# Block pairs 1 to 5 of tiles 2 to 6 by seven products; strided attention output in halves of one PSUM bank

## The chip, the cores and the metric

The kernel runs on one core of one Trainium2 chip. The metric is device time in microseconds (us) of one execution. All times are for the whole kernel; a profiled execution is also split by instruction and by engine: PE (matrix multiply), PEld (its weight loads), DVE (vector), ACT (scalar), POOL, and SP, which here only issues DMAs.

## What is computed

Sparse attention on 8 batches, 8 heads, 576 positions and a head size of 64, followed by a bilinear feed-forward layer on the 8 x 576 = 4608 tokens:

```python
mask_local = (rel >= 0) & (rel < 32)                                  # heads 0 to 3
mask_strided = (rel >= 0) & (pos[None, :] % 32 == pos[:, None] % 32)  # heads 4 to 7
scores = np.where(masks, scale * q @ k.T, -1e9)
attn = softmax(scores)
x = (attn @ v).transpose(0, 2, 1, 3).reshape(4608, 512)
out = ((x @ w_a) * (x @ w_b)) @ w_out        # w_a, w_b: 512 x 1536, w_out: 1536 x 512
```

## The kernel before

**Tiles and slots.** The feed-forward layer works on nine tiles of 512 tokens, t = 0 to 8. A tile has 16 slots: twelve for the blocks f of 128 of the 1536 columns (a and b are computed, and their product goes as bf16 into `pf`), and four for the output y. The attention of batch b is computed a tile ahead: its steps are spread over the slots of tile b-1. An order written out by hand decides where; each engine does its instructions in that order. `steps` maps a position to names of steps, `take(position)` issues them. A position is a slot (16t + slot, at the slot's end), or a place inside a slot: `("p", t, g)` late in block pair g, `("y", t, n)` after the n-th finished part of the output.

**Block pairs.** Blocks 2g and 2g+1 form pair g. An ordinary block takes four matmuls of 512 columns for a and four for b (L625), an ACT copy of a to SBUF (L646) and a DVE multiplication (L649). In tiles 2 to 6, pairs 1 to 4 (`MID_A`) go through `a_pair_mid`: the four matrix quarters of the pair's a come from seven products (of sums of quarters of x, in `xsum`, and of w_a, in `wsum_a`) instead of eight. A product is two matmuls of 256 columns, `P(...)` at L695; four products add up in the bank X, which ACT copies to SBUF after each (L721, L724, L731, L738), one is in Y and two are in Z. DVE adds the quarters (L717, three times a pair) and multiplies with the two banks b1 and b0 (L714, twice); b still takes eight matmuls of 512 columns (L709). Tiles 7 and 8 have a variant of their own, `a_pair`.

**PSUM banks.** `mm_bank` deals four banks in turn (three named mm and one named tp), so that a bank comes back after four. A pair takes four of them and the bank `e`; which of the five serves as X, Y, Z, b1, b0 changes with g in a cycle of three (L687). The output takes the next three.

**Attention steps of batch b in tile b-1.** Units u = 0 to 3 are the local heads, 4 to 7 the strided ones. `Q` copies transposed queries, `S` computes scores with their exponentials (on PE and ACT) and masks them (DVE); `s` and `m` are its two parts. `V` is the output. For u = 0 to 3: six matmuls into bank `o`, a reciprocal (L468), and a product into `xl` (L486), then by DMA (`O`, `I`) into `xT`. For u = 4 to 7, `step_VT`: eight matmuls of 72 columns (L519), four into `o` and four into `e`; on ACT a logarithm of each half (L531) and one exponential of both (L532), for the reciprocal of the sums; two DVE products into `xT` (L534). In tiles 2 to 6 the order is `PAIRED`, with V4 at slot 9, V5 at slot 11, and S7, V6 and V7 inside the output (`IN_Y`).

**Output.** y comes from seven products, too, on the two token halves i of `pf`, in two parts q each: 14 chains of six matmuls of 256 columns (L895), in the order `Y_ORDER`. Products 7, 6, 5 and 3 use the sums s2, s1, s0, s3 of `pf` quarters, which `fast_s` puts into `pss` on DVE (L829) piece by piece from slot 9 on. Products 1, 6, 5, 3 add up in one bank, 7 and 4 in a second, 2 is in a third; ACT copies after 1, 7, 6, 5 and 3 (L860, L866), DVE adds for 4, `+` and 2.

**The rest.** `wsum_make` (L668) makes the w_a sums on DVE: groups 1 to 4 in slots 17 to 19, groups 0 and 5 in slots 44 to 47. `pace` (L1146) is a one-element POOL copy of what the slot has finished: it holds back the DMAs that POOL issues behind it. SP issues the transposing loads (`step_D`: L322, L325, L328).

Of the kernel before, what the change touches and what calls it, by code (L numbers as in the profile page):

```python
# [7 lines left out]
F32 = mybir.dt.float32  # L8
BF16 = mybir.dt.bfloat16
# [7 lines left out]
RS = 8  # L17
# [10 lines left out]
FAST_Y = (1, 2, 3, 4, 5, 6, 7, 8)  # L28
MID_A = {t: (1, 2, 3, 4) for t in (2, 3, 4, 5, 6)}
FAST_A = {7: (1, 2, 3, 4, 5), 8: (0, 1, 2, 3, 4, 5)}  # L30
# [3 lines left out]
def kernel(  # L34
# [473 lines left out]
    def step_VT(b, u):  # L508

        c, half, M, n, G = unit(u)  # L510
        p = ps.pop((b, u))
        if "e" in psum4:
            o = [psum4[nm].tile([128, 512], F32, tag=nm, name=nm) for nm in "oe"]
        else:
            o2 = psum4["o"].tile([128, 2, 512], F32, tag="o", name="o")
            o = [o2[:, j] for j in range(2)]
        for j in range(2):
            for i in range(G):
                nc.tensor.matmul(o[j][:, i * n:(i + 1) * n], lhsT=vs_buf[b % 2][:, u - HL, 2 * i + j],  # L519
                                 rhs=p_cols(b, p, j, i, n, n)[:M], start=True, stop=True)  # L520
        r = sb.tile([128, RS * 4 * D], BF16, tag="xr", name="xr", bufs=2)[:64, :4 * W].bitcast(F32)
        by_token = lambda t: t.rearrange("d (p i j) -> d p i j", i=G, j=2)
        dst = xT[64 * (u % 2):64 * (u % 2) + 64, c, S * (b % XR):S * (b % XR + 1)]
        if "e" not in psum4:
            by_j = lambda t: t.rearrange("d j (i p) -> d p i j", p=NP)
            nc.scalar.activation(by_token(r), by_j(o2[64:, :, :W]), ACT.Ln)
            nc.scalar.activation(r, r, ACT.Exp, scale=-1.0)
            nc.vector.tensor_mul(by_token(dst), by_j(o2[:64, :, :W]), by_token(r))
            return
        for j in range(2):  # L530
            nc.scalar.activation(by_token(r)[:, :, :, j], o[j][64:, :W].rearrange("d (i p) -> d p i", p=NP), ACT.Ln)  # L531
        nc.scalar.activation(r, r, ACT.Exp, scale=-1.0)  # L532
        for j in range(2):
            nc.vector.tensor_mul(by_token(dst)[:, :, :, j], o[j][:64, :W].rearrange("d (i p) -> d p i", p=NP),  # L534
                                 by_token(r)[:, :, :, j])

# [29 lines left out]
    def F_mm(f, w, kk):  # L566
# [17 lines left out]
                 30: "V7"}}  # L584
    LATER = {-4: "Q0", -3: "Q1", -1: "S0", 0: "S1", 1: "V0", 2: "S2", 3: "V1 Q2 O0", 4: "S3 Q3", 5: "V2", 6: "S4", 7: "V3 O1 I0", 8: "S5", 9: "V4 I1",
             10: "S6",
             11: "V5"}
    IN_Y = {2: "S7", 6: "V6", 11: "V7"}
    PAIRED = {-4: "Q0", -3: "Q1", -1: "S0", 0: "S1", 1: "V0 Q2", 2: "s2", 3: "V1 Q3 O0", 4: "s3", 5: "V2", 6: "s4", 7: "V3 O1 I0", 8: "s5",
              9: "V4 I1", 10: "s6", 11: "m6 V5"}  # L590
    IN_P = {1: "m2", 2: "m3", 3: "m4", 4: "m5"}
    FN = {"Tk": step_Tk, "Tq": step_Tq, "S": step_S, "V": step_V, "X": step_X, "W": lambda b, n: fast_w(n, slice(0, 3)),
          "s": S_px, "m": S_m, "L": lead_vl, "O": rows_out, "I": rows_in, "Pk": lambda b, c: pair_up("k", c), "Pq": lambda b, c: pair_up("q", c),
          "Q": lambda b, n: step_Q(b, n // 2, n % 2)}
# [87 lines left out]
    def a_pair_mid(t, g):  # L682
# [47 lines left out]
        P(X, ws(0), xs(0))  # L730
        nc.scalar.copy(quarter(1, 1), X)  # L731
        P(Z, w(1, 1), xs(3))
        add(quarter(1, 0), Z)
# [6 lines left out]
        mult(0, b0)  # L740
        if g == 4:
            fast_s(t, 0, slice(0, 4))
        yield pf[:1, 2 * g, :1]
# [75 lines left out]
    def fast_s(t, n, gs):  # L819
        if t not in pss:  # L820
            pss[t] = nat.tile([128, FG * 5 * SW], BF16, tag="shared", name="ps").rearrange("p (n g m) -> p n g m", g=FG, n=5)
        s = pss[t][:, :, gs, :HT]
        x = pfs[t].rearrange("p (g e) (i m) -> p e i g m", e=2, i=2)[:, :, :, gs]
        a, b, op = ((x[:, 0, 1], x[:, 1, 1], ALU.add), (s[:, 0], x[:, 0, 0], ALU.subtract),
                    (x[:, 0, 0], x[:, 0, 1], ALU.subtract), (x[:, 1, 0], s[:, 1], ALU.subtract))[n]
        if (t, n) == (NT - 1, 2) and {gs.start, gs.start + 1} <= set(FAST_A[t]):
            later[t, gs.start] = lambda: nc.gpsimd.tensor_tensor(s[:, n], a, b, op=op)
            return
        nc.vector.tensor_tensor(s[:, n], a, b, op=op)  # L829
# [37 lines left out]

    Y_ORDER = [(x[0], int(x[1])) for x in "10 11 70 71 60 61 40 41 50 51 20 21 30 31".split()]
    TAIL_ORDER = [(x[0], int(x[1])) for x in "10 11 20 60 70 61 50 71 30 40 51 41 31 21".split()]

# [9 lines left out]
    def y_plan(t):  # L880
# [11 lines left out]

        for k, q, g in by_block(Y_ORDER, 2 if late else 0):
            b, lhs, rhs = plan[k]
            nc.tensor.matmul(bank[b][:, q], lhsT=lhs(g, q), rhs=rhs(g), start=k in "172" and q == 0 and g == 0,  # L895
                             stop=g == FG - 1, skip_group_check=True)
            if g == FG - 1:
                if q == 1:
                    y_post(k, y, slice(0, 2), bank[b])
                    if k == "5":  # L900
                        y_post("+", y, slice(0, 2), None)
                take(("y", t, Y_ORDER.index((k, q)) + 1))
            yield y
        do(16 * t + 19, store_half, 0)
# [34 lines left out]
    def ffn_ys(t, j, mid):  # L939
# [6 lines left out]
        if j == 3:  # L946
            for _ in yst[t]:
                pass
        return (y[0][:1, 0, :1], None, y[1][:1, 0, HN:HN + 1], y[1][:1, 0, :1])[j]

# [35 lines left out]
    with tc.manual_schedule(engines={ENG.PE, ENG.SP, ENG.Pool, ENG.DVE, ENG.Activation}):  # L986
# [78 lines left out]
        for b in range(1, B):  # L1065
            for pos, names in (STEPS.get(b) or {16 * (b - 1) + x: n for x, n in (PAIRED if b - 1 in MID_A else LATER).items()}).items():
                steps.setdefault(pos, []).append((b, names.split()))
            if b not in STEPS:
                for g in MID_A.get(b - 1, ()):
                    steps["p", b - 1, g] = [(b, IN_P[g].split())]  # L1070
                for n, names in IN_Y.items():
                    steps["y", b - 1, n] = [(b, names.split())]

# [5 lines left out]
        soon = {}  # L1079
        for t in FAST_Y[:-1]:  # L1080
            if t not in FAST_A:
                soon[16 * t + 10] = [lambda t=t: fast_s(t, 2, slice(4, 6))]
            soon[16 * t + 11] = [lambda t=t, n=n: fast_s(t, n, slice(4, 6)) for n in (0, 1)]
# [22 lines left out]
        for n in range(4):  # L1106
            do((17, 17, 18, 19)[n], wsum_make, n, slice(1, 5))
            do(16 * 2 + 12 + n, wsum_make, n, slice(0, 6, 5))
        for t in MID_A:
# [19 lines left out]
        for t in FAST_Y[:-1]:  # L1129
            for slot, n, z0, z1 in (  # L1130
                    ((8, 0, 0, 4),) if t == 1 else ()) + ((9, 2, 0, 4), (10, 1, 0, 4), (12, 3, 0, 6)) if t == 1 or t in MID_A else ((4, 0, 0, 2), (5, 2, 0, 2), (6, 1, 0, 2), (7, 3, 0, 2), (8, 2, 2, 4), (9, 0, 2, 4),
                                    (10, 1, 2, 4), (12, 3, 2, 6)):
# [47 lines left out]
```

## Time and profile before

| | |
|---|---|
| time, median of 3 runs | 321.34 us (319.42 to 321.73) |
| the profiled execution: time | 319.59 us |
| its span, first to last instruction | 317.9 us |
| granted PE clock, mean of the span | 0.997 |
| PE share of the chain that ended last | 84% |
| time of tiles 2, 3, 4, 5, 6 in the trace | 32.8, 32.9, 33.6, 32.9, 32.8 us |
| DVE busy in these tiles | 29.99, 30.44, 29.75, 29.78, 28.82 us |
| ACT busy in these tiles | 22.30, 22.41, 22.54, 22.38, 22.29 us |

The 1.7 us between span and time lie around the first and last instruction. [...]

### The profile page before, as it was taken

What the parts mean: (1) busy time and instruction counts of PE and PEld (TensorE: products, weight loads), DVE (VectorE), ACT (ScalarE), POOL (GpSimd) and SP (SyncE); (2) the same over time, 40 slices, a digit from 0 to 9 for tenths busy, and PEclk for the clock granted to TensorE, in tenths of its full rate; (3) what the DMA queues carried; (4) which work ended last, traced back from release to release, by engine and by line L of the source; (5) the groups of instructions that cost most, each with busy time, mean ns of one, the idle gap of its engine ahead of it and who ended that gap; (6) DMA issues with size and microseconds to landing.
All of it is one profiled execution on the core that took longest, in us unless ns stands there. A gap on an engine that the chain in (4) does not pass through costs nothing.

```text
span 317.9 us, 7371 instructions
## 1 busy us (share of the span) xinstructions
PE 310.7 (98%) x2798; PEld 220.7 (69%) x2798; DVE 263.9 (83%) x594; ACT 198.4 (62%) x414; POOL 111.5 (35%) x183
## 2 busy tenths in 40 slices
PE   8999999999999999999999999999999999999994
PEld 6754555455866687767988986769676966786684
DVE  5887876698979998999789978997899768857862
ACT  6964766455766776567756866586667755436541
POOL 8935712791264064205430445033101112203520
PEclk9999999999999999999999999999999999999998
DMA  8999999999999999999999999999252040004004
GB/s 152 172 205 194 204 186 204 220 98 165 115 134 169 251 119 78 129 92 209 147 157 230 130 90 102 96 226 155 26 154 58 0 133 2 2 0 133 2 0 134
DMA packets 127059, 40.32 MB, mean 127 GB/s; under 512 B 114864, under 2 KB 124144, under 8 KB 126832
## 3 DMA queue, kind: packets, MB, share of 16 engines
q0 software_dynamic: 79760, 19.20, 67.1%
q1 hardware_dynamic: 47120, 20.59, 35.9%
q8 instruction: 22, 0.36, 0.5%
q14 instruction: 13, 0.11, 0.2%
q10 hardware_dynamic: 144, 0.07, 0.1%
HBM read 38.93 MB, written 18.28 MB: 180 GB/s over the span
## 4 chain that ended last, share of the span: by engine, by line
PE 84%; DVE 6%; DMA 3%; POOL 2%; SPq 2%; issue 2%; ACT 1%; DVEq 0%; POOLq 0%
PE mm L895 19%; PE mm L625 18%; PE mm L709 8%; PE mm L695 6%; PE mm L775 6%; PE st L379 4%; PE mm L957 3%; PE ax L768 3%; PE e L695 2%; PE mm L768 2%; PE o L460 2%; DMA shared<-in_q_dram 2%; PE mm L922 2%; DMA qTs<-qr 2%; SPq L328 1%
## 5 line engine op out<-in xcount | busy, mean ns | idle before, releaser
L1146 POOL CAST pace<-pf 1x1 f32<-1x1 bf16 x47 | 15.2, 324 | 99.7 <-DVE pf L714 53.9
L625 PE MATMUL mm<-xT,wb_sb 128*128 128x512 bf16 (+1 forms) x192 | 47.4, 362 | 0.0
L625 PE MATMUL mm<-xT,wa_sb 128*128 128x512 bf16 (+1 forms) x192 | 47.4, 362 | 0.0
L399 ACT ACTIVATE p<-st 72x576 bf16<-72x576 f32 (+1 forms) x56 | 36.4, 650 | 9.2 <-PE st L379 8.2
L709 PE MATMUL mm<-xT,wb_sb 128*128 128x512 bf16 (+1 forms) x168 | 38.4, 343 | 0.0
L646 ACT COPY a_sb<-mm 128x512 f32<-128x512 f32 x44 | 25.7, 583 | 15.7 <-PE mm L625 14.9
L895 PEld LDWEIGHTS <-ps 128*128 128x128 bf16 x336 | 32.7, 98 | 3.7
L625 PEld LDWEIGHTS <-wb_sb 128*128 128x128 bf16 x192 | 18.2, 98 | 16.9 <-DMA wb_sb<-in_moe_w_b_dram 0.5
L895 PE MATMUL mm<-wf,ps 128*128 128x256 bf16 x252 | 29.8, 273 | 0.0
L860 ACT COPY y_sb<-mm 128x512 f32<-128x512 f32 (+1 forms) x32 | 17.9, 558 | 19.0 <-PE mm L895 16.4
L649 DVE TENSOR_TENSOR pf<-a_sb,mm 128x512 bf16<-128x512 f32 x34 | 23.1, 680 | 5.9 <-ACT a_sb L646 5.7
L775 PE MATMUL mm<-xT,wb_sb 128*128 128x512 bf16 x88 | 26.2, 379 | 0.0
L625 PEld LDWEIGHTS <-wa_sb 128*128 128x128 bf16 x192 | 17.4, 98 | 12.4
L1146 POOL COPY pace<-y_sb 1x1 f32<-1x1 f32 x22 | 8.4, 380 | 49.5 <-DVE y_sb L858 27.0
L895 PEld LDWEIGHTS <-pf 128*128 128x128 bf16 x252 | 23.5, 98 | 2.7
L709 PEld LDWEIGHTS <-wb_sb 128*128 128x128 bf16 x192 | 18.7, 97 | 7.4
L714 DVE TENSOR_TENSOR pf<-a_sb,mm 128x512 bf16<-128x512 f32 x35 | 22.7, 683 | 0.5
L238 POOL DMA_DIRECT2D vs<-in_v_dram x24 | 21.7, 907 | 3.9 <-issue 1.6
L895 PE MATMUL mm<-wo_sb,pf 128*128 128x256 bf16 x168 | 21.8, 273 | 0.0
L829 DVE TENSOR_TENSOR ps<-pf 128x512 bf16<-128x512 bf16 (+2 forms) x37 | 17.8, 481 | 0.7
L417 DVE TENSOR_TENSOR p<-p,mask_l 128x576 int16<-128x576 int16 x32 | 14.4, 450 | 2.2 <-ACT p L399 2.0
L460 PEld LDWEIGHTS <-p 128*128 128x128 bf16 (+1 forms) x256 | 12.9, 97 | 4.7 <-DVE p L417 1.3
(222 smaller groups left out, 735.8 us busy)
## 6 DMA issues: line engine op xcount, KB each, us to landing
out_dram<-y_sb SPq DMA_DIRECT2D x14, 512.0 KB, 5.2
kr<-in_k_dram POOLq DMA_DIRECT2D x12, 288.0 KB, 6.8
qr<-in_q_dram POOLq DMA_DIRECT2D x12, 288.0 KB, 8.1
vl<-in_v_dram POOLq DMA_DIRECT2D x6, 384.0 KB, 8.8
out_dram<-y_sb SPq DMA_DIRECT2D x7, 256.0 KB, 4.4
vs<-in_v_dram POOLq DMA_DIRECT2D x24, 72.0 KB, 5.7
xd<-xl SPq DMA_DIRECT2D x12, 144.0 KB, 5.0
wo_sb<-in_moe_w_out_dram POOLq DMA_DIRECT2D x4, 384.0 KB, 12.0
```

Source lines behind the costliest of these rows:

```text
L238: nc.gpsimd.dma_start(out=vs_buf[b % 2][:, h, :, 0:D], in_=v[b, HL + h].rearrange("(p r) d -> p r d", r=RS))
L399: nc.scalar.activation(p_flat(p)[:M, :2 * W].rearrange("p (i n) -> p i n", n=2 * n), st[:M].rearrange("p a (i n) -> p (a i) n", n=256)[:, ...
L460: nc.tensor.matmul(of[:, j, i, :w], lhsT=pt, rhs=vt, start=True, stop=True)
L625: nc.tensor.matmul(ps_[:, c0:c0 + n], lhsT=w[:, kk, 128 * f:128 * (f + 1)], rhs=xT[:, kk, x0:x0 + n], start=(kk == first and c0 == 0), sto ...
L646: nc.scalar.copy(a_sb, ab[0])
L649: nc.vector.tensor_mul(pf[:, f, :].rearrange("p (i a s) -> p a i s", i=2, s=16), halves(a_sb), halves(ab[1]))
L695: nc.tensor.matmul(bank, lhsT=lhs(c), rhs=rhs(c), start=start and c == 0, stop=c == 1, skip_group_check=True)
L709: nc.tensor.matmul(dst, lhsT=wb_sb[:, kk, 128 * f:128 * (f + 1)], rhs=rhs, start=kk == 0 and k in (None, 0), stop=kk == KD - 1 and k in (N ...
L714: nc.vector.tensor_mul(pf[:, 2 * g + e, :].rearrange("p (i a s) -> p a i s", i=2, s=16), halves(a[e]), halves(bank))
L775: nc.tensor.matmul(got[e], lhsT=wb_sb[:, kk, 128 * f:128 * (f + 1)], rhs=xT[:, kk, x0:x0 + TTOK], start=kk == 0, stop=kk == KD - 1)
L895: nc.tensor.matmul(bank[b][:, q], lhsT=lhs(g, q), rhs=rhs(g), start=k in "172" and q == 0 and g == 0, stop=g == FG - 1, skip_group_check=True)
L1146: nc.gpsimd.tensor_copy(pace, done)
```

## The change

Five things. (1) Pair 5 of tiles 2 to 6 also goes through `a_pair_mid`. (2) In these tiles the outputs of the strided units are computed in halves: `VT_p` does four matmuls into one bank (`o` or `e`), one logarithm and one exponential, `VT_n` one DVE product. There are eight halves; they stand inside pairs 4 and 5 (`("q", t, g)`, a new place behind the copy of the X bank's third product) and inside the output, at `("m", t, n)`, after n output matmuls. (3) The output's products come in another order, `MID_ORDER`: product 2's first part is drawn forward beside product 1. (4) The sums of `pf` are made in five larger instructions instead of seven; s0 and s3 are made inside the output, and s1 is formed from s2. Q0 and Q1 move to places inside the output of the tile before. `pace` looks at the two halves of y in the other order. (5) The w_a sums of group 5 are made together with those of groups 1 to 4.

```diff
@@ -26,7 +26,7 @@
 FAST_Y = (1, 2, 3, 4, 5, 6, 7, 8)
-MID_A = {t: (1, 2, 3, 4) for t in (2, 3, 4, 5, 6)}
+MID_A = {t: (1, 2, 3, 4, 5) for t in (2, 3, 4, 5, 6)}
 FAST_A = {7: (1, 2, 3, 4, 5), 8: (0, 1, 2, 3, 4, 5)}
@@ -509,11 +509,8 @@
         p = ps.pop((b, u))
-        if "e" in psum4:
-            o = [psum4[nm].tile([128, 512], F32, tag=nm, name=nm) for nm in "oe"]
-        else:
-            o2 = psum4["o"].tile([128, 2, 512], F32, tag="o", name="o")
-            o = [o2[:, j] for j in range(2)]
+        o2 = psum4["o"].tile([128, 2, 512], F32, tag="o", name="o")
+        o = [o2[:, j] for j in range(2)]
         for j in range(2):
@@ -521,18 +518,31 @@
         dst = xT[64 * (u % 2):64 * (u % 2) + 64, c, S * (b % XR):S * (b % XR + 1)]
-        if "e" not in psum4:
-            by_j = lambda t: t.rearrange("d j (i p) -> d p i j", p=NP)
-            nc.scalar.activation(by_token(r), by_j(o2[64:, :, :W]), ACT.Ln)
-            nc.scalar.activation(r, r, ACT.Exp, scale=-1.0)
-            nc.vector.tensor_mul(by_token(dst), by_j(o2[:64, :, :W]), by_token(r))
-            return
+        by_j = lambda t: t.rearrange("d j (i p) -> d p i j", p=NP)
+        nc.scalar.activation(by_token(r), by_j(o2[64:, :, :W]), ACT.Ln)
+        nc.scalar.activation(r, r, ACT.Exp, scale=-1.0)
+        nc.vector.tensor_mul(by_token(dst), by_j(o2[:64, :, :W]), by_token(r))
+
+    def VT_p(b, u, h, nm):
+
+        c, half, M, n, G = unit(u)
+        p = ps[b, u]
+        o = psum4[nm].tile([128, 512], F32, tag=nm, name=nm)
         for j in range(2):
-            nc.scalar.activation(by_token(r)[:, :, :, j], o[j][64:, :W].rearrange("d (i p) -> d p i", p=NP), ACT.Ln)
+            for i in range(2):
+                nc.tensor.matmul(o[:, (2 * j + i) * n:(2 * j + i + 1) * n], lhsT=vs_buf[b % 2][:, u - HL, 2 * (2 * h + i) + j],
+                                 rhs=p_cols(b, p, j, 2 * h + i, n, n)[:M], start=True, stop=True)
+        r = sb.tile([128, RS * 4 * D], BF16, tag="xr", name="xr", bufs=2)[:64, :2 * W].bitcast(F32)
+        nc.scalar.activation(r, o[64:, :W], ACT.Ln)
         nc.scalar.activation(r, r, ACT.Exp, scale=-1.0)
-        for j in range(2):
-            nc.vector.tensor_mul(by_token(dst)[:, :, :, j], o[j][:64, :W].rearrange("d (i p) -> d p i", p=NP),
-                                 by_token(r)[:, :, :, j])
+        held[b, "vt", u, h] = o, r
+
+    def VT_n(b, u, h):
+
+        o, r = held.pop((b, "vt", u, h))
+        by_j = lambda t: t.rearrange("d (j i p) -> d p i j", j=2, p=NP)
+        dst = xT[64 * (u % 2):64 * (u % 2) + 64, unit(u)[0], S * (b % XR):S * (b % XR + 1)]
+        nc.vector.tensor_mul(dst.rearrange("d (p i j) -> d p i j", i=4, j=2)[:, :, 2 * h:2 * h + 2], by_j(o[:64, :W]), by_j(r))
 
@@ -582,15 +592,16 @@
                  30: "V7"}}
-    LATER = {-4: "Q0", -3: "Q1", -1: "S0", 0: "S1", 1: "V0", 2: "S2", 3: "V1 Q2 O0", 4: "S3 Q3", 5: "V2", 6: "S4", 7: "V3 O1 I0", 8: "S5", 9: "V4 I1",
-             10: "S6",
-             11: "V5"}
-    IN_Y = {2: "S7", 6: "V6", 11: "V7"}
-    PAIRED = {-4: "Q0", -3: "Q1", -1: "S0", 0: "S1", 1: "V0 Q2", 2: "s2", 3: "V1 Q3 O0", 4: "s3", 5: "V2", 6: "s4", 7: "V3 O1 I0", 8: "s5",
-              9: "V4 I1", 10: "s6", 11: "m6 V5"}
+    PAIRED = {-1: "S0", 0: "S1", 1: "V0 Q2", 2: "s2", 3: "V1 Q3 O0", 4: "s3", 5: "V2", 6: "s4", 7: "V3 O1 I0", 8: "s5",
+              9: "na4 I1", 10: "s6", 11: "nb4"}
     IN_P = {1: "m2", 2: "m3", 3: "m4", 4: "m5"}
+    IN_Q = {4: "va4", 5: "vb4"}
+    IN_Y = {8: "vc5", 12: "s7", 14: "na5 m6", 24: "vb5", 26: "nb5 f0 m7", 34: "vc6", 36: "na6 f3", 44: "vb6", 46: "nb6", 56: "vc7",
+            58: "na7", 67: "vb7", 69: "nb7"}
     FN = {"Tk": step_Tk, "Tq": step_Tq, "S": step_S, "V": step_V, "X": step_X, "W": lambda b, n: fast_w(n, slice(0, 3)),
-          "s": S_px, "m": S_m, "L": lead_vl, "O": rows_out, "I": rows_in, "Pk": lambda b, c: pair_up("k", c), "Pq": lambda b, c: pair_up("q", c),
+          "s": S_px, "m": S_m, "va": lambda b, u: VT_p(b, u, 0, "o"), "vc": lambda b, u: VT_p(b, u, 0, "e"),
+          "vb": lambda b, u: VT_p(b, u, 1, "o"), "na": lambda b, u: VT_n(b, u, 0), "nb": lambda b, u: VT_n(b, u, 1),
+          "f": lambda b, n: fast_s(b - 1, n, slice(0, FG)), "L": lead_vl, "O": rows_out, "I": rows_in, "Pk": lambda b, c: pair_up("k", c), "Pq": lambda b, c: pair_up("q", c),
           "Q": lambda b, n: step_Q(b, n // 2, n % 2)}
@@ -729,6 +740,7 @@
         nc.scalar.copy(quarter(1, 1), X)
+        take(("q", t, g))
         P(Z, w(1, 1), xs(3))
@@ -738,8 +750,6 @@
         mult(0, b0)
-        if g == 4:
-            fast_s(t, 0, slice(0, 4))
         yield pf[:1, 2 * g, :1]
@@ -823,6 +833,8 @@
                     (x[:, 0, 0], x[:, 0, 1], ALU.subtract), (x[:, 1, 0], s[:, 1], ALU.subtract))[n]
+        if n == 1 and t in MID_A:
+            a, b = x[:, 1, 1], s[:, 2]
         if (t, n) == (NT - 1, 2) and {gs.start, gs.start + 1} <= set(FAST_A[t]):
@@ -866,6 +878,7 @@
     Y_ORDER = [(x[0], int(x[1])) for x in "10 11 70 71 60 61 40 41 50 51 20 21 30 31".split()]
+    MID_ORDER = [(x[0], int(x[1])) for x in "10 11 20 70 71 60 61 40 41 50 51 21 30 31".split()]
     TAIL_ORDER = [(x[0], int(x[1])) for x in "10 11 20 60 70 61 50 71 30 40 51 41 31 21".split()]
@@ -890,7 +903,7 @@
 
-        for k, q, g in by_block(Y_ORDER, 2 if late else 0):
+        for m, (k, q, g) in enumerate(by_block(MID_ORDER, 3) if t in MID_A else by_block(Y_ORDER, 2 if late else 0)):
             b, lhs, rhs = plan[k]
@@ -900,6 +913,7 @@
                 take(("y", t, Y_ORDER.index((k, q)) + 1))
+            take(("m", t, m + 1))
             yield y
@@ -946,7 +960,8 @@
                 pass
-        return (y[0][:1, 0, :1], None, y[1][:1, 0, HN:HN + 1], y[1][:1, 0, :1])[j]
+        ends = y[1][:1, 0, HN:HN + 1], y[1][:1, 0, :1]
+        return (y[0][:1, 0, :1], None, *(ends[::-1] if t in MID_A else ends))[j]
 
@@ -1063,13 +1078,15 @@
         for b in range(1, B):
-            for pos, names in (STEPS.get(b) or {16 * (b - 1) + x: n for x, n in (PAIRED if b - 1 in MID_A else LATER).items()}).items():
+            t = b - 1
+            for pos, names in (STEPS.get(b) or {16 * t + x: n for x, n in PAIRED.items()}).items():
                 steps.setdefault(pos, []).append((b, names.split()))
             if b not in STEPS:
-                for g in MID_A.get(b - 1, ()):
-                    steps["p", b - 1, g] = [(b, IN_P[g].split())]
-                for n, names in IN_Y.items():
-                    steps["y", b - 1, n] = [(b, names.split())]
+                for kind, where in (("p", IN_P), ("q", IN_Q), ("m", IN_Y)):
+                    for x, names in where.items():
+                        steps.setdefault((kind, t, x), []).append((b, names.split()))
+                for x, pos, nm in ((28, 47, "Q0"), (29, 60, "Q1")):
+                    steps.setdefault(("m", t - 1, pos) if t - 1 in MID_A else x, []).append((b, [nm]))
 
@@ -1078,6 +1095,8 @@
         for t in FAST_Y[:-1]:
+            if t in MID_A:
+                continue
             if t not in FAST_A:
@@ -1104,8 +1123,8 @@
         for n in range(4):
-            do((17, 17, 18, 19)[n], wsum_make, n, slice(1, 5))
-            do(16 * 2 + 12 + n, wsum_make, n, slice(0, 6, 5))
+            do((17, 17, 18, 19)[n], wsum_make, n, slice(1, 6))
+            do(16 * 2 + 12 + n, wsum_make, n, slice(0, 1))
         for t in MID_A:
@@ -1128,7 +1147,8 @@
             for slot, n, z0, z1 in (
-                    ((8, 0, 0, 4),) if t == 1 else ()) + ((9, 2, 0, 4), (10, 1, 0, 4), (12, 3, 0, 6)) if t == 1 or t in MID_A else ((4, 0, 0, 2), (5, 2, 0, 2), (6, 1, 0, 2), (7, 3, 0, 2), (8, 2, 2, 4), (9, 0, 2, 4),
+                    (8, 0, 0, 4), (9, 2, 0, 4), (10, 1, 0, 4), (12, 3, 0, 6)) if t == 1 else (
+                    (9, 2, 0, 4), (11, 2, 4, 6), (11, 1, 0, 6)) if t in MID_A else ((4, 0, 0, 2), (5, 2, 0, 2), (6, 1, 0, 2), (7, 3, 0, 2), (8, 2, 2, 4), (9, 0, 2, 4),
                                     (10, 1, 2, 4), (12, 3, 2, 6)):
```

## The prediction

> **What bounds the kernel now.** I read the page's busy line first, then the windows by tile, then PE's instructions in order of time.
>
> ```profile
> PE 310.7 (98%) x2798; PEld 220.7 (69%) x2798; DVE 263.9 (83%) x594; ACT 198.4 (62%) x414; POOL 111.5 (35%) x183
> ```
>
> 98% may hide pauses, as a matmul's recorded time overlaps the next. The windows (length, then busy time of PE, PEld, DVE, ACT and POOL, clock, DMA) are tiles 1, 3, 4 and 5:
>
> ```profile
> 56.30:90.80 34.50, 34.37 (x272) 21.54 (x270) 30.17 (x56) 20.25 (x35) 16.84 (x28) 1.00 1.39 148
> 123.60:156.50 32.90, 32.90 (x292) 23.70 (x290) 30.44 (x69) 22.41 (x50) 11.57 (x19) 1.00 1.38 130
> 156.50:190.10 33.60, 33.37 (x354) 29.79 (x353) 29.75 (x67) 22.54 (x50) 11.24 (x19) 1.00 1.33 156
> 190.10:223.00 32.90, 32.90 (x291) 23.75 (x290) 29.78 (x67) 22.38 (x50) 11.25 (x19) 1.00 1.37 142
> ```
>
> Tiles 3 and 5 last 32.9 us each, with PE at full clock and never idle. Tile 4 is longer: DVE waited there for a DMA (its wait is in brackets), and PE then lost 0.3 and 0.26 us.
>
> ```profile
> 163.12 0.45 DVE L335 COPY qz1s<-qTs 64x1152 bf16<-64x1152 bf16 x1 [0.94 <-DMA qTs<-qr]
> ```
>
> PE in order of time, in tile 3 (start, duration, instruction), gives the rates from start to start:
>
> ```profile
> 142.32 1.03 PE L625 MATMUL mm<-xT,wa_sb 128*128 128x512 bf16 x4
> 143.19 1.03 PE L625 MATMUL mm<-xT,wb_sb 128*128 128x512 bf16 x4
> ...
> 146.29 1.48 PE L895 MATMUL mm<-wo_sb,pf 128*128 128x256 bf16 x12
> 147.60 0.41 PE L379 MATMUL st<-qz0s,kT0s 128*128 128x144 bf16 x4
> ```
>
> Four of 512 columns take 0.87 us, 0.216 each; twelve of 256 take 1.31, 0.109 each. So in tiles 2 to 6 PE's columns are the bound: a gain must be fewer columns, and every new PE wait counts in full.
>
> **The change part by part. (1) Pair 5.** Before: 16 matmuls x 0.216 = 3.46 us. After: 14 x 0.109 + 8 x 0.216 = 3.26. (Pair 2 of tile 3 confirms it: 131.18 to 134.69, less 0.25 for scores.) This is -0.20 a tile, **-1.0 us** over five.
> [...]
> Beside PE: three DVE additions more (0.41 us each, 0.34 from start to start) and five ACT copies of 0.37 in place of two of 0.58. The five larger sums cost DVE 0.68 + 0.42 + 3 x 0.94 = 3.92, against 0.68 x 3 + 0.42 x 3 + 0.94 = 4.24 for the seven. DVE goes from 29.8 to about 30.6 of 32.9 us: cover, if the order fits.
>
> **(2) The border of pairs 4 and 5.** Bank X of pair 4 is the bank that pair 5 takes as b1. X is free when ACT has copied its fourth product. The same reuse in tile 5, pairs 2 and 3:
>
> ```profile
> 200.95 0.38 PE L695 MATMUL e<-xT,tq 128*128 128x256 bf16 x2
> ...
> 201.17 0.35 PE L460 MATMUL o<-vl,p 128*128 128x65 bf16 x6
> ...
> 201.35 0.60 PE L695 MATMUL mm<-xT,wa_sb 128*128 128x256 bf16 x4
> ...
> 201.37 0.37 ACT L738 COPY a_sb<-e 128x256 f32<-128x256 f32 x1 [0.60 <-PE e L695]
> ...
> 201.79 0.81 PE L709 MATMUL e<-xT,wb_sb 128*128 128x512 bf16 x3
> ```
>
> The product starts at 200.95, its copy 0.42 later, and ends at 0.79; b1 comes at 0.84. It doesn't wait, because the V step's 0.18 us stand in between. Between pairs 4 and 5 no V step stands any more (it moves into the pairs), so b1 is due at 0.22 + 0.44 = 0.66, before the copy has ended. What a release costs is shown in tile 1, where PE waits for a mask:
>
> ```profile
> 71.30 0.44 DVE L417 TENSOR_TENSOR p<-p,mask_l 128x576 int16<-128x576 int16 x1
> ...
> 71.80 0.24 PEld L460 LDWEIGHTS <-p 128*128 128x128 bf16 x6 [0.62 <-DVE p L417]
> ```
>
> 71.74 to 71.80 is 0.06. So PE waits 0.79 + 0.06 - 0.66 = 0.19 us a tile, **+0.95 us** (0.13 to 0.25 a tile, 0.65 to 1.25). Behind it stand all later matmuls. ACT isn't late for this copy: the new logarithm and exponential (0.43 each by L531's rows) fit between two copies 1.1 us apart.
>
> **(3) V4's first half** stands inside pair 4, when bank `o` has only just been freed by L486. L486 ends 0.00 to 0.08 us before PE would come (107.89 against 107.89 in tile 2; 207.17 against 207.25 in tile 5), so with 0.06 for the release: 0 to 0.1 a tile, **+0.1 us** (0 to 0.5).
>
> **(4) The output stage**, by hand from its start, with the durations of before. DVE: pair 5's multiplications end at 1.3 (its extra queue, a half's product and a 0.68 sum, is cleared before). The first use of block 10 is due at 1.8, after the 15 matmuls drawn forward: no wait. s2 is ready at 2.0, due at 2.8; s1 at 2.9, due at 3.8. ACT needs 0.87 for a half, so V5's second half is through at 4.2 and its product ends at 4.7; then s0 is ready at 5.6, due at 6.7; s3 at 7.2, due at 8.9. Banks `o` and `e` are free 0.3 to 0.7 early each time. One wait is new: product 3 needs product 5's copy. It now has six matmuls and a half V between (0.65 + 0.13 = 0.78) instead of twelve and a whole; the copy needs 0.2 + 0.58 and the release 0.06: 0.05 a tile, **+0.25 us** (0 to 0.5).
> Q0 and Q1 end 0.9 us before the scores that use them. The last xT columns are written at 10.3, due at 11.7.
>
> **(5) The w_a sums of tile 1.** L668 takes 0.69 for four groups and 0.41 for two, 0.14 a group; four instructions with five groups cost DVE 0.55 more. DVE runs without a pause from 58.6 to 77, and PE waited there for it (0.29 at 71.8, 0.09 at 74). So nothing hides it: **+0.5 us** (0 to 0.55). The same groups leave the output of tile 2, where DVE has room: nothing.
>
> **(6) Pace and SP.** SP's order is the same. The copy that the next k and q loads wait for comes about 0.7 us earlier, as it watches an earlier product. That may end tile 4's wait or not: **-0.2 us** (-0.56 to 0).
>
> Sum: -1.0 + 0.95 + 0.1 + 0.25 + 0.5 - 0.2 = +0.6 us. On the profiled 319.59 that is 320.2; the median of the runs stands 1.75 higher, so 321.34 + 0.6 = **321.9**. It is no change within what a measurement of this kernel can tell, 1% (3.2 us; the three runs spread over 2.3).
>
> **The rivals.** *No wait at the border* (0.16). If b1's bank were free in time, (2) drops out: 321.0. For it: the other four borders show none. Against: it is arithmetic on rows 0.05 us wide of the wait.
> *DVE's queue in pair 5 and the output* (0.13). The order has 0.5 us of room for block 10 and 1.1 for s0. From there each 0.1 us of lateness costs 0.5 over five tiles; 0.5 us too late gives 324.4. For it: DVE is at 91% and takes in 0.8 more; for a half's product it can stand 0.6 us before s0. Against: in pairs 1 and 4 DVE still idles 0.2.
> *ACT bounds the output* (slower, 0.05). If a half costs what a unit cost whole (0.33 + 0.44 + 0.68 = 1.45), six halves, five copies and one exponential need 8.7 + 2.9 + 0.65 = 12.2 us in a stage of 10.2: +2.0 a tile, 331.7 us. It decides from 1.1 us a half on. Against: half the columns took 0.43.
> *Weight loads* (slower, 0.02). Each 256-column product has its own load of 98 ns under 109 ns of streaming; if half of the loads showed, 70 x 0.049 = +3.4 us, 325.3. [...] Against: 84 such matmuls in a row of the output keep 0.109.
> That the change isn't made can't be: the built order has the fifth pair.
>
> **How the numbers follow.** The sum's case keeps 0.64. The terms' ends give 321.34 - 0.9 = 320.4 and 321.34 + 1.8 = 323.1; without (2) and (5), and with tile 4's gain, 319.8. With DVE's case the upper end is 324.4; the runs themselves spread by 1.9 below the median. Range 319.3 to 324.6. Below 318.1 nothing in the sum reaches, only a low measurement: faster 0.04. Slower, above 324.55: half of DVE's case, ACT, weight loads: 0.14. Within 1%: 0.82.
>
> **What would show it.** Pair 5 from first product to last at 3.26 less its additions; a PE wait of about 0.19 on ACT's L738 at the first b1 matmul of pair 5, five times; tile 2 to 6 windows of 32.8 to 33.0; tile 1 at about 35.0. I am wrong if these tiles get shorter by over 0.3 us, or if PE waits for a `pf` or `ps` of DVE in the output.

## The result, and the profile after

| | before | after |
|---|---|---|
| median of 6 runs each | 319.84 us (319.08 to 321.73) | 324.67 us (322.83 to 326.71) |
| the profiled execution: time, span | 319.59, 317.9 us | 323.36, 321.6 us |
| tile 1 in the trace | 34.36 us | 34.84 us |
| tiles 2 to 6 together | 164.94 us | 168.17 us |

The ratio is 1.0146, 95% interval 1.0105 to 1.0187: slower by more than 1%, where no change was forecast, and 0.07 us above the range. Three of the changed kernel's six executions (325.98 to 326.71 us) ran at a mean clock of 0.987 to 0.989 and took 3 us more than the other three (322.83 to 323.36 us, 0.998 to 1.000), and as in a trace of such an execution (e12's) the granted clock is 0.81 to 0.84 from 10 to 30 us, ahead of tile 1, and full behind it, the tiles are compared below. The median lies between these two groups, and its 0.07 us say little; what is to be explained is how far the traces lie from the sum.

A tile is counted here from its first matmul of a to that of the next tile; the prediction's window of tile 1 ended 0.14 us later (34.50 instead of 34.36).

The traces differ by 3.7 us in span, where the sum had 0.6. The page's first part, and the windows by tile of the changed kernel (length, busy time of PE, PEld, DVE, ACT, POOL, clock, DMA), tiles 1, 3, 4 and 5:

```profile
PE 310.7 (97%) x2788; PEld 222.6 (69%) x2820; DVE 275.6 (86%) x599; ACT 206.5 (64%) x449; POOL 113.5 (35%) x182
```

```profile
56.35:91.19 34.84, 34.24 (x269) 21.36 (x270) 30.52 (x56) 20.11 (x35) 16.92 (x28) 1.00 1.40 150
125.18:158.90 33.72, 33.16 (x293) 24.11 (x296) 32.50 (x70) 24.05 (x56) 11.75 (x19) 1.00 1.50 141
158.90:192.54 33.64, 33.24 (x352) 29.65 (x351) 32.23 (x68) 24.00 (x56) 11.42 (x19) 1.00 1.38 141
192.54:226.08 33.54, 32.92 (x294) 24.19 (x295) 32.19 (x68) 23.99 (x56) 12.07 (x19) 1.00 1.31 139
```

PE's recorded busy time is the same to 0.1 us: the time is in pauses of PE. DVE went from 29.8 to 32.2 us in tile 5, not to the 30.6 of the working. Read from start to start (two starts, less 0.216 us for 512 columns or 0.109 for 256), the new pauses in tiles 2 to 6 are: before unit 6's first half 2.13 us in all, before pair 5's b1 1.36, before the V half inside pair 4 0.50, before product 3 0.19, at the end of tile 2's output and in the first blocks of tile 3 0.64. Tile 4's old 0.56 and the columns of pair 5 (1.0) go off: 4.82 - 1.56 = 3.26, against 3.23 measured for the five tiles. Tile 1 adds 0.48, and 3.23 + 0.48 are the 3.7.

The largest one, in tile 5, whose output starts at 215.13 (all engines by start; only DVE and PE shown):

```profile
215.11 1.50 DVE L725 TENSOR_TENSOR pf<-a_sb,mm 128x512 bf16<-128x512 f32 x2
...
216.53 0.65 DVE L545 TENSOR_TENSOR xT<-o,xr 64x288 bf16<-64x288 f32 x1
...
217.10 0.41 DVE L841 TENSOR_TENSOR ps<-pf 128x512 bf16<-128x512 bf16 x1
...
217.54 0.96 DVE L841 TENSOR_TENSOR ps<-pf,ps 128x1536 bf16<-128x1536 bf16 x1
...
218.27 1.26 PE L908 MATMUL mm<-wf,ps 128*128 128x256 bf16 x10
218.53 0.63 DVE L545 TENSOR_TENSOR xT<-e,xr 64x288 bf16<-64x288 f32 x1
219.19 0.46 DVE L417 TENSOR_TENSOR p<-p,mask_s 72x576 int16<-72x576 int16 x1
...
219.80 0.29 PE L533 MATMUL e<-p,vs 72*128 72x72 bf16 x4 [0.27 <-DVE p L417]
```

Ten matmuls from 218.27 on end their turn at 219.36; unit 6's half comes at 219.80. It waits for its mask, and DVE has no pause of more than 0.03 us in front of that: two multiplications, a half's product, two sums, a half's product, the mask. The bracket (0.27) counts from the recorded end of the last matmul; PE lost 0.43. The waits view names the same five waits, too small for that reason:

```profile
PE e L533 <- DVE p L417: 1.3, 5, 0.3
```

Two rows are nowhere near what the working took for them. The groups by shape, before and after (mean ns of one):

```profile
L534 DVE TENSOR_TENSOR xT<-o,xr 64x288 bf16<-64x288 f32 x20 | 9.5, 475 | 7.5 <-ACT xr L532 7.4
L534 DVE TENSOR_TENSOR xT<-e,xr 64x288 bf16<-64x288 f32 x20 | 9.2, 462 | 0.0
```

```profile
L545 DVE TENSOR_TENSOR xT<-o,xr 64x288 bf16<-64x288 f32 x25 | 15.9, 637 | 0.3
L545 DVE TENSOR_TENSOR xT<-e,xr 64x288 bf16<-64x288 f32 x15 | 9.6, 637 | 0.3
```

The half's product (L545) has the same 288 elements as before's (L534) and takes 0.637 us instead of 0.47: eight a tile, 1.3 us.

The border of pairs 4 and 5 in tile 2, the copy of pair 4's X bank and the first matmul of b1:

```profile
109.78 0.38 PE L706 MATMUL mm<-xT,tq 128*128 128x256 bf16 x2
...
110.00 0.38 PE L706 MATMUL mm<-xT,wa_sb 128*128 128x256 bf16 x2
110.22 0.38 PE L706 MATMUL e<-xT,wa_sb 128*128 128x256 bf16 x2
110.23 0.37 ACT L750 COPY a_sb<-mm 128x256 f32<-128x256 f32 x1
...
110.66 0.81 PE L720 MATMUL mm<-xT,wb_sb 128*128 128x512 bf16 x3
```

b1 was due at 110.44, the copy ends at 110.60, 0.06 later b1 starts: the wait of the working, 0.22 here instead of 0.19. In the other tiles it is 0.24 to 0.31, as ACT, still at the half's exponential, begins this copy up to 0.1 later. In tile 5 ACT goes from pair 4's third copy to this one without a pause:

```profile
210.22 0.36 ACT L742 COPY a_sb<-mm 128x256 f32<-128x256 f32 x1
210.61 0.41 ACT L536 ACTIVATE xr<-o 64x288 f32<-64x288 f32 x1
211.04 0.44 ACT L537 ACTIVATE xr<-xr 64x288 f32<-64x288 f32 x1
211.51 0.37 ACT L750 COPY a_sb<-mm 128x256 f32<-128x256 f32 x1
```

Tile 4's DMA wait has gone: the copy that carried the 0.94 us bracket has none.

```profile
164.59 0.44 DVE L335 COPY qz1s<-qTs 64x1152 bf16<-64x1152 bf16 x1
```

### The profile page after: what moved, and what is told of

It is laid out like the page before. It is cut to its first block, busy times and chain, and to the rows that moved or that the text cites. A ratio compares the mean times of both kernels' runs of the same rounds, so it can differ in the third digit from the quotient of the medians.

```text
span 321.6 us, 7460 instructions
## 1 busy us (share of the span) xinstructions
PE 310.7 (97%) x2788; PEld 222.6 (69%) x2820; DVE 275.6 (86%) x599; ACT 206.5 (64%) x449; POOL 113.5 (35%) x182
## 3 DMA queue, kind: packets, MB, share of 16 engines
q1 hardware_dynamic: 47120, 20.59, 34.9%
## 4 chain that ended last, share of the span: by engine, by line
PE 86%; DVE 6%; ACT 3%; issue 2%; DMA 2%; POOL 0%; DVEq 0%; POOLq 0%; ACTq 0%
PE mm L908 18%; PE mm L636 16%; PE mm L720 11%; PE mm L706 7%; PE mm L785 5%; PE st L379 4%; PE e L706 4%; PE mm L972 3%; PE ax L778 3%; PE o L460 2%; PE mm L778 2%; DVE p L417 2%; DMA shared<-in_q_dram 2%; PE mm L936 2%; PE e L720 1%
## 5 line engine op out<-in xcount | busy, mean ns | idle before, releaser
L1166 POOL CAST pace<-pf 1x1 f32<-1x1 bf16 x43 | 17.2, 400 | 97.3 <-DVE pf L725 62.3
L636 PE MATMUL mm<-xT,wa_sb 128*128 128x512 bf16 (+1 forms) x135 | 35.8, 366 | 0.2
L908 PEld LDWEIGHTS <-ps 128*128 128x128 bf16 x336 | 31.8, 98 | 3.7
L908 PE MATMUL mm<-wf,ps 128*128 128x256 bf16 x252 | 32.0, 272 | 0.0
L657 ACT COPY a_sb<-mm 128x512 f32<-128x512 f32 x34 | 19.8, 583 | 12.7 <-PE mm L636 12.4
L785 PE MATMUL mm<-xT,wb_sb 128*128 128x512 bf16 x83 | 25.3, 379 | 0.1
L908 PE MATMUL mm<-wo_sb,pf 128*128 128x256 bf16 x168 | 23.2, 273 | 0.0
L636 PEld LDWEIGHTS <-wa_sb 128*128 128x128 bf16 x144 | 13.2, 98 | 10.4
L537 ACT ACTIVATE xr<-xr 64x288 f32<-64x288 f32 x40 | 17.7, 444 | 1.3
L841 DVE TENSOR_TENSOR ps<-pf 128x512 bf16<-128x512 bf16 (+3 forms) x32 | 16.9, 530 | 0.5
```

Source lines behind the costliest of these rows:

```text
L636: nc.tensor.matmul(ps_[:, c0:c0 + n], lhsT=w[:, kk, 128 * f:128 * (f + 1)], rhs=xT[:, kk, x0:x0 + n], start=(kk == first and c0 == 0), sto ...
L657: nc.scalar.copy(a_sb, ab[0])
L785: nc.tensor.matmul(got[e], lhsT=wb_sb[:, kk, 128 * f:128 * (f + 1)], rhs=xT[:, kk, x0:x0 + TTOK], start=kk == 0, stop=kk == KD - 1)
L1166: nc.gpsimd.tensor_copy(pace, done)
```

## The experiments

Each kernel changes the changed kernel (323.36 us profiled; tiles 2 to 6: 168.17 us), unless it says otherwise. The experiments ran in four groups (e1 to e4, e5 to e8, e9 and e10, e11 and e12), each on another chip beside runs of the kernel before. So a time is set against before by its ratio, and the kernels are set against each other by the tiles in their traces.

**e1: the mask ahead of a product.**

```diff
-    IN_Y = {8: "vc5", 12: "s7", 14: "na5 m6", 24: "vb5", 26: "nb5 f0 m7", 34: "vc6", 36: "na6 f3", 44: "vb6", 46: "nb6", 56: "vc7",
+    IN_Y = {8: "vc5", 12: "s7", 14: "m6 na5", 24: "vb5", 26: "nb5 f0 m7", 34: "vc6", 36: "na6 f3", 44: "vb6", 46: "nb6", 56: "vc7",
```

> Only the order on DVE is changed: in the output of tiles 2 to 6 unit 6's mask goes ahead of unit 5's first half product. Theory 'load': DVE has no idle time from pair 4 to there, so the product that is now last becomes what PE waits for (bank e, L545); the wait before unit 6's first half falls from 0.42 to about 0.2 us a tile, some -1.0 us of the changed kernel's 323.4. Theory 'order': only the mask stood in a wrong place; the wait goes to 0, -2.1 us.

322.80 us (median of 4), tiles 2 to 6 167.56. The wait is 0.21 to 0.23 us in all five tiles, as "load" had it: now the product is last.

```profile
217.46 0.45 DVE L417 TENSOR_TENSOR p<-p,mask_s 72x576 int16<-72x576 int16 x1
...
217.94 0.63 DVE L545 TENSOR_TENSOR xT<-e,xr 64x288 bf16<-64x288 f32 x1
218.50 0.63 DVE L545 TENSOR_TENSOR xT<-o,xr 64x288 bf16<-64x288 f32 x1
...
218.62 0.29 PE L533 MATMUL e<-p,vs 72*128 72x72 bf16 x4
```

Only 0.6 us came out, not 1.0: tile 2 had two other waits, 0.27 us behind its first pair, for a DMA (`vl`), and 0.24 instead of 0.03 before unit 7, about what the tile had gained at unit 6.

**e2: a sum on POOL.**

```diff
-        nc.vector.tensor_tensor(s[:, n], a, b, op=op)
+        eng = nc.gpsimd if t in MID_A and gs == slice(0, 4) else nc.vector
+        eng.tensor_tensor(s[:, n], a, b, op=op)
```

> In tiles 2 to 6 the first piece of s2 (0.68 us on DVE) is made on POOL, the order is left. Theory 'load': DVE is 0.6 us earlier behind it, the wait of unit 6's first half (0.42) is gone in all five tiles and the waits at the end of tile 2's output get shorter: -2.1 to -2.7 us. Rival 'order': nothing but the mask's place counts, and the mask is still last: within 0.3 us of the changed kernel. Rival 'POOL late': POOL took 0.67 us for 256 elements, so some 2.7 us for 1024; if it stands behind a wait, PE waits for ps at product 7 and the time gets longer.

332.86 us (median of 4): 9.5 us longer, by none of the three accounts. DVE and POOL in tile 2, and in tile 6:

```profile
113.22 2.80 DVE L728 TENSOR_TENSOR a_sb<-p,a_sb 128x256 f32<-128x256 f32 x1
113.59 2.13 POOL L842 TENSOR_TENSOR ps<-pf 128x1024 bf16<-128x1024 bf16 x1
...
116.05 1.29 DVE L725 TENSOR_TENSOR pf<-a_sb,mm 128x512 bf16<-128x512 f32 x2
...
116.80 0.28 PE L909 MATMUL mm<-wo_sb,pf 128*128 128x256 bf16 x1 [1.72 <-DVE pf L725]
```

```profile
255.96 2.12 POOL L842 TENSOR_TENSOR ps<-pf 128x1024 bf16<-128x1024 bf16 x1
256.17 0.41 DVE L728 TENSOR_TENSOR a_sb<-mm,a_sb 128x256 f32<-128x256 f32 x1
257.18 0.42 DVE L728 TENSOR_TENSOR a_sb<-mm,a_sb 128x256 f32<-128x256 f32 x1 [0.61 <-ACT p L399]
257.52 0.84 DVE L728 TENSOR_TENSOR a_sb<-p,a_sb 128x256 f32<-128x256 f32 x1
```

The same addition takes 0.415 us on average in the changed kernel. The one with both inputs in SBUF (`p7`, which the lines call p, and `a_sb`) ends 0.3 us after POOL's recorded end in each of the five tiles: 2.80 us in tile 2, 2.7 to 3.0 in tiles 3 to 5, 0.84 in tile 6, where it comes late in POOL's span. In tile 6 two additions with one input in PSUM run while POOL works and keep 0.41 and 0.42. Pair 5's multiplications and the output's first use of block 10 stand behind the held addition. The trace shows which addition is long beside POOL's, in all five tiles, and until when; by what it is held isn't shown. In tiles 2 to 5 DVE's record starts 0.3 to 0.6 us ahead of POOL's (113.22 against 113.59 in tile 2), and its addition is long all the same. Whether POOL's recorded starts are late isn't known.

**e3: scores at the border.** Unit 6's score matmuls go from inside pair 5 to slot 9 (`h` is `S_p`, `x` is `S_x`).

```diff
-              9: "na4 I1", 10: "s6", 11: "nb4"}
+              9: "h6 na4 I1", 10: "x6", 11: "nb4"}
```

> The four score matmuls of unit 6 (0.25 us of PE) stand between pairs 4 and 5 and no longer inside pair 5; their exponential stays. Theory 'too little cover': pair 5's b1 waited 0.22 to 0.31 us for ACT's copy of pair 4's last product only because nothing stands in between; the wait falls to 0 to 0.06 a tile, -1.2 us. Rival: ACT is simply late in pair 5, and PE loses the same at pair 5's next product of bank X, behind ACT's first copy: no change. The wait before unit 6's first half in the output is the same by both, or a little longer, as PE comes there earlier and DVE does not: then up to 1.2 us go back.

324.34 us (median of 4), tiles 2 to 6 167.57. b1's wait fell to 0 to 0.07 us as "cover" had it, and 0.19 us came up in each tile at X's third product, near to what the rival said, though for another reason:

```profile
212.50 0.38 PE L706 MATMUL e<-xsum,tq 128*128 128x256 bf16 x2
...
212.91 0.37 ACT L735 COPY a_sb<-e 128x256 f32<-128x256 f32 x1 [0.54 <-PE e L706]
...
213.34 0.38 PE L706 MATMUL e<-xsum,tk 128*128 128x256 bf16 x2
```

ACT isn't late here: it waits itself for X's second product (0.41 us after its start) and copies 0.37. From one product to the next the copied bank needs 0.84 us here, and PE had only 0.65 of work left for it once the scores were away. The 0.25 us of cover can stand in one place only. Unit 6's wait is 0.35 to 0.37 us, shorter by 0.05 to 0.08, where the same or more was expected.

**e4: the weight sums later.**

```diff
-            do((17, 17, 18, 19)[n], wsum_make, n, slice(1, 6))
-            do(16 * 2 + 12 + n, wsum_make, n, slice(0, 1))
+            do((17, 17, 18, 19)[n], wsum_make, n, slice(1, 5))
+            do((31, 32, 32, 33)[n], wsum_make, n, slice(5, 6))
+            do(16 * 7 + 12 + n, wsum_make, n, slice(0, 1))
```

> The w_a sums of group 5 are made at the start of tile 2 (slots 31 to 33), where DVE idled 1.3 us, and those of group 0 in tile 7's output, instead of tile 1 and the output of tile 2. Theory: DVE's backlog in tile 1 cost 0.47 us and the four sums in tile 2's output, 0.28 us each, the 0.6 us of waits there that tiles 3 to 6 do not have; both go: -1.0 us. Rival: the waits at the end of tile 2's output have another cause: -0.5 us.

323.02 us (median of 4). Tile 1 lost 0.47 us (34.37), and the waits at tile 2's end are gone, so both parts of the theory hold; but four additions at the start of tile 2 made two new waits of 0.34 and 0.29 us in pairs 2 and 3, where PE waits for DVE's multiplications of the pair before. Tiles 2 to 6 stay at 168.28.

**e5: another walk of the product.** Inputs in stored order, the output written with the stride.

```diff
-        by_j = lambda t: t.rearrange("d (j i p) -> d p i j", j=2, p=NP)
+        by_j = lambda t: t.rearrange("d (j i p) -> d j i p", j=2, p=NP)
...
-        nc.vector.tensor_mul(dst.rearrange("d (p i j) -> d p i j", i=4, j=2)[:, :, 2 * h:2 * h + 2], by_j(o[:64, :W]), by_j(r))
+        nc.vector.tensor_mul(dst.rearrange("d (p i j) -> d j i p", i=4, j=2)[:, :, 2 * h:2 * h + 2], by_j(o[:64, :W]), by_j(r))
```

> Only the order in which L545 walks its 288 elements is changed: both inputs are read in their stored order (j, i, p) and the output is written with the stride, instead of all three in the output's order (p, i, j). Same operation, same place. Theory 'mis-sized product': these 40 instructions take 0.637 us each where before's took 0.47 for the same 288 elements, and this is what fills DVE's queue; they fall to 0.47 or less, DVE's busy time in a tile goes from 32.2 to 31 us or less, the 0.42 us wait before unit 6's first half ends in all five tiles, and tile 2's waits at its end (0.6) with it; b1's waits (0.22 to 0.31) stay: 323.4 - 2.1 - 0.6 = 320.7 us. Rival: the length does not come from the walk; 0.63 stays and so does the time.

350.71 us (median of 4): the walk does decide, and this one is worse.

```profile
L545 DVE TENSOR_TENSOR xT<-o,xr 64x288 bf16<-64x288 f32 x25 | 35.9, 1438 | 0.3
...
L545 DVE TENSOR_TENSOR xT<-e,xr 64x288 bf16<-64x288 f32 x15 | 21.4, 1428 | 0.3
```

5.0 ns an element, with every bf16 result 16 bytes from the last and both inputs now read in order. So what had to be asked next was which of the three operands costs 0.16 us in the changed kernel.

**e6, e7: cover at both places, and sums in tile 1.** Both rest on e5's product, so their times (352.12 and 349.79 us, medians of 4 and 6) say nothing of the sum; single waits still do. e6 takes the scores behind pair 5's first X product and draws a b0 matmul forward:

```diff
         nc.scalar.copy(quarter(0, 0), X)
+        take(("x", t, g))
         b_mm(b1, 1, (0, 1, 2))
...
         b_mm(b1, 1, (3,))
+        if g == 5:
+            b_mm(b0, 0, (0,))
...
-        b_mm(b0, 0, range(KD))
+        b_mm(b0, 0, range(g == 5, KD))
```

> The walk of e5, and in pair 5 cover at both places where bank X is copied: unit 6's score matmuls (0.25 us) go between pair 5's first product of X and b1, and the first of b0's four matmuls (0.22 us) goes ahead of X's third product. Theory 'cover': with both, neither b1 (0.22 to 0.31) nor X's third product (0.19 where the scores were taken away alone) waits: 1.2 us less than e5, some 319.5 us. Rival: DVE or ACT is the bound by then, and the same time comes back before the output: within 0.4 us of e5.

b1 waits 0 to 0.06 us, X's third product not at all: "cover" holds for the two places. e7 adds e4's edit to e6, with `do((25, 26, 26, 27)[n], wsum_make, n, slice(5, 6))` as its second new line:

> As e6, and the w_a sums of group 5 in slots 25 to 27 of tile 1, behind DVE's backlog and ahead of a stretch where it idled 0.95 us, those of group 0 in tile 7's output. Theory: tile 1 loses its 0.49 us wait, nothing new: 319.0 us, 0.2% under before or the same as before. Rival: the sums only move the backlog (as at slots 31 to 33, where two waits of 0.34 and 0.29 came up): within 0.3 us of e6.

Tile 1 takes 34.37 us (34.84 in e6), with no new wait in it.

**e8: pair 5 as ordinary blocks.** `MID_A` back to pairs 1 to 4, the halves kept.

```diff
-    IN_Q = {4: "va4", 5: "vb4"}
+    IN_Q = {4: "va4"}
...
-              9: "na4 I1", 10: "s6", 11: "nb4"}
+              9: "na4 I1", 10: "s6", 10.5: "vb4", 11: "nb4"}
```

> The changed kernel with pair 5 as two ordinary blocks (four matmuls of 512 columns for a and four for b each); halves, output order and sums of the changed kernel stay; unit 4's second half stands in block 11. Theory 'DVE's load': the three additions fall away (1.0 us of DVE a tile), so the 0.42 wait ends, and with it b1's; pair 5 takes 0.2 us more: -2.1 - 1.4 + 1.0 = -2.5, 320.9 us. Rival: the halves alone make DVE late: the wait of about 0.4 stays, and the time is 323.0.

324.63 us (median of 4), tiles 2 to 6 168.67. The rival holds as to the wait: without the three additions DVE's busy time in tile 5 is 31.0 us instead of 32.2, and the wait is 0.50 to 0.52 us. It isn't DVE's total that makes the mask late, but what stands between pair 5's last multiplication and the mask, and there the halves' products were not touched.

**e9: the reciprocals stored in the output's order.**

```diff
-        nc.scalar.activation(r, o[64:, :W], ACT.Ln)
+        nc.scalar.activation(r.rearrange("d (p i j) -> d p i j", i=2, j=2), o[64:, :W].rearrange("d (j i p) -> d p i j", j=2, p=NP), ACT.Ln)
...
-        nc.vector.tensor_mul(dst.rearrange("d (p i j) -> d p i j", i=4, j=2)[:, :, 2 * h:2 * h + 2], by_j(o[:64, :W]), by_j(r))
+        nc.vector.tensor_mul(dst.rearrange("d (p i j) -> d p i j", i=4, j=2)[:, :, 2 * h:2 * h + 2], by_j(o[:64, :W]), r.rearrange("d (p i j) -> d p i j", i=2, j=2))
```

> Only the storage of a half's reciprocals is changed: ACT's logarithm (L536) writes them in the output's order (p, i, j), so that L545 reads them one behind the other; its other input and its output are walked as in the changed kernel (write in runs of four). Theory: before's products took 0.47 us because their reciprocals lay two elements apart; the changed kernel's take 0.637 because each element read lies 288 bytes or more from the last. L545 falls to about 0.47, DVE is 1.3 us a tile less busy, the wait before unit 6's first half (0.42) falls to 0 to 0.1 in all five tiles and tile 2's waits at its end are halved: 1.6 to 2.4 us less than the changed kernel's 323.4. The logarithm may grow from 0.41 to 0.43. Rival: it is the output in runs of four that costs; 0.63 stays, and so does the time.

320.68 us (median of 10; ratio to before 1.0038, 1.0002 to 1.0073), tiles 2 to 6 166.07. The groups, and tile 5:

```profile
L545 DVE TENSOR_TENSOR xT<-o,xr 64x288 bf16<-64x288 f32 x25 | 11.2, 446 | 0.9 <-ACT xr L537 0.2
L545 DVE TENSOR_TENSOR xT<-e,xr 64x288 bf16<-64x288 f32 x15 | 6.7, 448 | 0.3
```

```profile
190.75:223.90 33.15, 32.80 (x293) 24.19 (x295) 30.92 (x68) 24.01 (x57) 11.79 (x20) 1.00 1.28 143
```

0.637 became 0.447, DVE's tile 32.2 became 30.9, the wait 0.43 became 0.05 or less, and tile 2's end has none but product 3's. (The 166.07 still hold one wait of 0.45 us for a DMA of `vl`, behind tile 2's first pair, that the changed kernel has not.) DVE's total is that of e8 (31.0), where the wait is 0.5: the two kernels differ in what stands ahead of the mask. The logarithm stayed at 0.41. b1's wait is still 0.26 to 0.31. By the distance from one reciprocal read to the next, the product took 0.637 us at 288 bytes or more (the changed kernel), 0.47 at 8 (before) and 0.447 at 4 (e9); with the results written 16 bytes apart (e5) it took 1.43. Only 0.637 against 0.447 is a change of one operand alone; before and e5 walk the PSUM input and the output otherwise, too. Why the distance costs this isn't shown.

**e10: all repairs**, the edits of e1 and e9, the cover of e6 and the sums of e7 together, without e5's walk.

> e9, and: the mask of unit 6 ahead of unit 5's first half (as e1); cover at both places in pair 5 (as e6); the w_a sums of group 5 in slots 25 to 27, of group 0 in tile 7's output (as e7). Theory: the five things that cost time are each gone: -2.1 (unit 6), -1.2 (b1), -0.5 (tile 1), -0.6 (tile 2's end) from 323.4, so 319.0 in a profiled run, against 319.6 of before: 0.2% faster. Rival: DVE, 31 of 32.8 us busy, gives a part back in another place; 320 us or more, no better than before.

319.02 us (median of 12), ratio to before 0.9993 (0.9959 to 1.0027): the same. Tiles 2 to 6 take 164.46 us, tile 1 34.36. No wait is left over 0.15 us in tiles 2 to 6; the small ones are 0.46 us in five tiles for bank `o` inside pair 4, 0.24 before product 3, 0.17 at b1, 0.17 before unit 5's first half in `e`: 1.04 together. Tile 5, which took 32.90 us before and 33.54 in the changed kernel:

```profile
189.25:222.15 32.90, 32.69 (x293) 24.27 (x295) 30.82 (x68) 23.89 (x57) 11.84 (x20) 1.00 1.32 143
```

**e11: e10 with pair 5 as ordinary blocks** (e8's edit).

> e10, but pair 5 of tiles 2 to 6 as two ordinary blocks, and unit 6's scores back inside it. Theory: with the waits gone what is left of pair 5 is its columns, 0.20 us a tile as the rates said: +1.0 us, less 0.2 of small waits in pair 5 of e10, so some 0.8 us over e10, 319.5 in a profiled run against 318.7. Rival: the three additions and five copies still cost what the columns save; the same as e10 within 0.3 us.

320.19 us (median of 12), ratio to before 1.0007 (0.9977 to 1.0037); tiles 2 to 6 165.55, 1.09 us more than in e10. 0.43 of that are two waits at the border of ordinary blocks (0.22 in tile 3, 0.21 in tile 4, which e8 has as well), and e10's waits at b1 and before unit 5, 0.34, are not in it: 1.09 - 0.43 + 0.34 = 1.0 for the columns, as the rates have it.

**e12: more of tile 1's sums later**, `slice(1, 4)` in slots 17 to 19 and `slice(4, 6)` in slots 25 to 28.

> e10, and group 4's w_a sums also leave slots 17 to 19 of tile 1; groups 4 and 5 are made together in slots 25 to 28. Theory: DVE is 0.5 us earlier in the first half of tile 1, and its two waits of 0.30 and 0.09 us for a mask, which the kernel before has as well, end: -0.4 us against e10, 318.3 in a profiled run. Rival: four instructions of 0.41 us do not fit where DVE idled 0.95 us, and PE waits in the second half of tile 1: no gain.

319.71 us (median of 12), ratio 0.9994 (0.9955 to 1.0032); tile 1 34.20 us, 0.16 less than e10. One of the two waits shrank from 0.30 to 0.14, the other stayed at 0.09; neither ended, and the ratio can't be told from e10's.

## Why the prediction failed

**(1)** held: pair 5 in tile 2 runs from 110.00 to 113.86, less 0.25 (scores), 0.13 (V half) and 0.22 (wait): 3.26, as worked out; e10 against e11 shows the 1.0 us in the tiles of their traces, though not in their times, whose ratios to before overlap. The 256-column products keep their 0.109 us (twelve of tile 5's output take 1.31 us, from 216.83 to 218.14).

**(2)** was the right mechanism, mis-sized: 1.36 us for 0.95, above the 1.25 of its range. The working fitted a logarithm and an exponential, 0.86 us, between two copies "1.1 us apart". By the rows of before that is from start to start (207.78 to 208.75 in tile 5, and 0.13 for the half's matmuls), and the first copy itself takes 0.36 of it: 0.74 was left, so the second copy had to be some 0.1 late, as it was (the lines of ACT above: no pause over 0.03 us from the first copy to the second). e3 and e6 show the cause of the wait by giving the cover back.

**(3)** came out at the upper end, 0.50 us for 0.1.

**(4)** is the step that failed. It priced a half's product "with the durations of before", by a row of the same operation, element count and engine; what differed, and decided, was the layout of one input. Eight products a tile at 0.637 instead of 0.47 add 1.3 us, and two of them stand between pair 5 and unit 6's mask. Where the walk had "banks `o` and `e` are free 0.3 to 0.7 early each time", unit 6's first half came 0.42 to 0.44 late, five times. e9 changes that layout alone and the wait goes.

The layout isn't the whole of it. Two products make 0.33 us, which doesn't turn 0.3 early into 0.43 late, and in e9 unit 6's first half is still 0.03 to 0.05 late and not early. Three more terms of the walk were too small, by the rows of tile 5. The multiplications end 1.48 us after the output's start instead of 1.3 (the second waited 0.12 for an ACT copy, L750). Three instructions behind them, the second sum, the half's product and the mask, start 0.03 after the end of the one before, where the overlap of the first sum with the product ahead of it (217.10 against 217.18) would have them start 0.08 ahead: 0.33 in all. And PE's matmul starts 0.15 us after the mask's recorded end, in each of the five tiles, where 0.06 was taken for a release. With the products that is 0.93, the way from 0.5 early to 0.43 late. No kernel changed these three alone. The walk also has no line for unit 6's mask, and so its sign of being wrong, a wait for `pf` or `ps`, missed the wait that came.

The statement that DVE reaches 30.6 us fails in the main for the same reason: with the layout mended it is 30.9. The rival of DVE's queue, with its 0.5 us for each 0.1 of lateness, describes what happened (0.43 gives 2.1). The walk's new wait, product 3's, is there at 0.05 in four of the five tiles. The rivals of ACT and of weight loads are out: the tiles last 33.3 to 34.0 us, not 34.9, ACT is busy for 24 of them, and 256 columns keep their 0.109 us.

**(5)** held in tile 1 (0.47 for 0.5, by e4 and e7) but not in tile 2's output, where the four sums of group 0 were said to cost nothing: 0.64 us of waits, gone in e4 when the sums leave, and in e9 with the sums still there: the longer products had spent DVE's room.

**(6)** The wait of tile 4 is gone, 0.56 us, the term's far end. No trace of e8 to e12 has it either. Why is open: neither `pace` nor the order of the loads was changed alone.

So 3.7 us are two causes in the main: a layout (e9 takes back 2.1 of the 3.2 us of tiles 2 to 6) and cover missing at one border. With both mended, pair 5 saves its 1.0 us, and small waits at the halves, at pair 5's border and before product 3 return 1.04. That e10's tiles are still 0.48 us below before's is the DMA wait of tile 4; whether the other runs of before have that wait isn't known, as only one has a trace, and by the medians the two kernels are the same.

## What to carry to other kernels

A row of the profile prices an instruction only for the same access patterns: compare strides of each input and of the output, not the element count alone (288 elements took 0.447 to 1.43 us here), and bound the price by other rows when one of them changes. Walk a saturated engine's queue from the last late input to the deadline; the engine's total said nothing about it here (DVE at 31.0 us a tile in e8 and 30.9 in e9, the wait 0.5 us and 0.05 or less). When work is moved away from between two uses of a bank, ask what covered the copy there (here 0.18 us of a V step, and without it PE waited 0.22 to 0.31).

## What was not expected of the hardware

Beside one POOL addition of 2.13 us a DVE addition with both inputs in SBUF took 2.80 us in tile 2, where its mean in the changed kernel is 0.415, while two with an input in PSUM kept 0.41 and 0.42 in tile 6 (e2). And one instruction of 288 elements cost 0.637 or 0.447 us by the layout of one input in SBUF alone (e9), and 1.43 when all three operands were walked in another order, the output with a stride of 16 bytes (e5).
